# Merging the scores of two key chunks into 136 columns in a banded-attention stage

## The chip, the cores and the metric

The kernel runs on one core of a Trainium2 chip. Five engines work side by side, each in the order in which its instructions were written: TensorE (PE in the profile, its weight loads PEld), VectorE (DVE), ScalarE (ACT), GpSimd (POOL) and SyncE (SP, which issues transfers). The metric is the device time of one execution in microseconds. Three runs of the kernel before gave 881.18, 882.76 and 883.11 us; the median is 882.76.

## The reference

```python
scores = scale * np.matmul(q, k.transpose(0, 1, 3, 2))     # 2 x 8 heads, 768 x 768, head size 64
is_sink = pos[None, :] < 4
rel = pos[:, None] - pos[None, :]
keep = is_sink | ((rel >= 0) & (rel < 128))
a = softmax(np.where(keep, scores, -1e9))
attn = np.matmul(a, v)
x = attn.transpose(0, 2, 1, 3).reshape(1536, 512)
x = sum_e p[:, e] * (relu(x @ w1[e]) @ w2[e])              # 4 experts
out = gate * (relu(x @ w1b[top]) @ w2b[top])               # 8 experts, the best one for each token
```

A query sees the 128 keys up to its own and the first 4 keys. For a tile of 128 queries these lie in two chunks of 128 keys: its own chunk (key column no greater than the query's row) and the one before it (key column greater than the row).

## The kernel before

The attention stage (`narrow_path`) works on 8 pairs of heads, g = 0 to 7, and in each on 6 query tiles, i = 0 to 5, and two heads, `par` = 0 and 1. For each (g, i, par) TensorE computes the scores of 264 key columns into a PSUM bank (`scores`, line 370: the chunk before, the tile's own chunk and 8 sink columns). VectorE adds a mask and takes the row's minimum of the negated scores (`mask_max`, line 383), ScalarE takes the exponential and its sum (`exp`, line 389), VectorE makes the reciprocal (lines 402, 403), and GpSimd scales the row (`norm`, line 408; for the last pair VectorE too).

The probabilities are then transposed by TensorE, by key chunk c: `pt_pe` transposes what tile c has in its own chunk (line 415) and what tile c+1 has in that chunk (line 417), for both heads, four blocks of 128x128 for c = 0 to 4 and two for c = 5. ScalarE or VectorE copies them out of PSUM (`pt_ev`, line 420, tile `ptx`, four buffers), and `av` (line 454) multiplies them with the values. The sink columns go another way (`sink_cp`, `sink_pe`, `sink_ev`, `av_sink`). `x_hi` and `x_lo` (lines 469, 473) write the result for the experts. The transposed queries and keys of the next pair (lines 324 to 347) and a few casts of expert weights (lines 678, 682, on GpSimd) are worked in between.

What stands in which order on the engines is set by the class `Order`: every step has a rank (`RANK`, tuned numbers), a cost in microseconds per engine that may run it, and steps that it waits for; a list planner takes them one by one and writes them out. PSUM has two buffers for scores and two for transposed blocks. After the last pair TensorE goes on at once with the experts, whose order the planner does not set.

Of the kernel before, what the change touches and what calls it, by code (L numbers as in the profile page):

```python
# [19 lines left out]
P = 128  # L20
# [16 lines left out]
VAR = [0, 1, 2, 3, 2, 3]  # L37
SPLIT3 = ((0, 0), (0, 1), (1, 0))
RANK = dict(
    sc=-1.86, mask=-1.68, exp=2.32, recip=1.03, norm=5.82, scp=-0.61, spe=2.96, sev=1.51, pt=2.75, ev=6.07, av=6.4, avs=4.76, xhi=11.43,  # L40
    xlo=1.57, qpe=-6.05, qhi=-8.82, qlo=-11.56, kpe=-4.73, khi=-2.69, klo=1.91, qld=-11.4, kld=-11.4, vld=-7.72, vsl=-4, wld=0, Lpt=5.73, Lsc=-2.22,
    Lav=8.22, Lexp=-2.63, Lnorm=3.72, Lkpe=-4.67, Lavs=11.14, Lrecip=2.17, Lxlo=5.65, Lkhi=-5.14, Lxhi=9.92, Lev=6.37, Lscp=-0.42,
    Lsev=1.82,
)
SLACK = dict(PE=0.02, ACT=0.17, DVE=0.06, POOL=0, SP=0)
GROUP = ((0, 1), (1, 2), (2, 3), (3, 4), (4, 5), (5, 6))
# [160 lines left out]
class Attention:  # L207


    def __init__(s, tc, st, c0, ps, q, k, v, n_sink, window, x, ident):  # L210
# [3 lines left out]
        nc = s.nc  # L214
        c1 = st.enter_context(tc.tile_pool(name="a1", bufs=1))
# [8 lines left out]
        V, A, G = nc.vector, nc.scalar, nc.gpsimd  # L224
# [15 lines left out]
        e = c1.tile([1, 1], F32, name="warm")  # L240
# [10 lines left out]
        s.masks = c1.tile([P, 4, W], F32, name="masks")  # L251
# [5 lines left out]
        G.memset(s.masks[:, 1, 2 * P :], -1.0e30)  # L257
        s.q_pe(0, s.pp[:, 0], 0)
        s.busy(s.xo[1], 6)
        s.k_pe(0, s.xo[0], 0)  # L260
# [25 lines left out]
    def make_masks(s, pool):  # L286

        V, A, masks = s.nc.vector, s.nc.scalar, s.masks
        win = pool.tile([P, 2 * P], F32, name="win")
        snk = pool.tile([P, P], F32, name="snk")  # L290
        V.tensor_scalar(win, s.rel, s.wf, -1.0e30, ALU.is_ge, ALU.mult)
        V.tensor_scalar(snk, s.key, s.nsf, -1.0e30, ALU.is_ge, ALU.mult)
        V.tensor_tensor(masks[:, 0, :P], win[:, P:], snk, ALU.max)
        V.tensor_tensor(masks[:, 1, :P], win[:, :P], snk, ALU.max)
        A.copy(masks[:, 1, P : 2 * P], win[:, P:])
        A.copy(masks[:, 2, : 2 * P], win)
        A.copy(masks[:, 2, 2 * P :], snk[:, :NS])
        A.copy(masks[:, 3, :P], win[:, :P])
        A.copy(masks[:, 3, P : P + NS], snk[:, :NS])
        A.copy(masks[:, 3, P + NS :], win[:, P:])  # L300

    def load(s, g, n, z=slice(0, 6)):
        b, h0 = divmod(g * 2, H)
# [44 lines left out]

    def narrow_path(s, ctx, late, parts):

        tc, nc, ident = s.tc, s.nc, s.ident
        c1 = ctx.enter_context(tc.tile_pool(name="b1", bufs=1))
        vsr, pp, vt = s.vsr, s.pp, s.vt
        NP = NPAIR
        masks, sk = s.masks, s.sk
        skT = [c1.tile([P, P], F32, name=f"skT{n}") for n in range(2)]
        V, A, G = nc.vector, nc.scalar, nc.gpsimd
# [6 lines left out]
        def scores(g, i, par):  # L364
            t = pr[g]
            qs, kk = s.qs[g % 2], s.kk[g % 2].rearrange("p s a c -> p s (a c)")
            z = slice(par * HD, (par + 1) * HD)
            sc = ps1.tile([P, 512], F32, tag="sc", name="sc")
            for n, (x, y) in enumerate(SPLIT3):
                nc.tensor.matmul(  # L370
                    sc[:, :W], qs[z, x, i * P : (i + 1) * P], kk[z, y, START[i] : START[i] + W], start=(n == 0), stop=(n == 2)
                )
            t["sc", par] = sc

        def mask_max(g, i, par):
            t = pr[g]
            if i == 0 and par == 0:
                t["P"] = hp_.tile([P, 2, 6, W], F32, tag="P", name="P")
                t["nm"] = sm.tile([P, 2, 6], F32, tag="nm", name="nm")
                t["su"] = sm.tile([P, 2, 6], F32, tag="su", name="su")  # L380
            m = sm.tile([P, W], F32, tag="m", name="m")
            t["m", par, i] = m
            V.tensor_tensor_reduce(  # L383
                m, t["sc", par][:, :W], masks[:, VAR[i]], -1.0, 3.0e38, ALU.add, ALU.min, t["nm"][:, par, i : i + 1]
            )

        def exp(g, i, par):
            t = pr[g]
            A.activation(  # L389
                t["P"][:, par, i],  # L390
                t["m", par, i],
                AF.Exp,
                scale=-1.0,
                bias=t["nm"][:, par, i : i + 1],
                accum_out=t["su"][:, par, i : i + 1],
            )
# [7 lines left out]

        def norm(g, a, b, par, eng):
            t = pr[g]
            y = t["P"][:, par, a:b]
            eng.tensor_tensor(y, y, t["r", a][:, par].unsqueeze(2).to_broadcast([P, b - a, W]), ALU.mult)  # L408
# [12 lines left out]

        def pt_ev(g, c, eng):
            n = 2 * P if c < 5 else P
            px = sm.tile([P, 2, 2 * P], F32, tag="ptx", name="ptx")
            pr[g]["ptx", c] = px
            copy(eng, px[:, :, :n], pr[g]["pt", c][:, :, :n])

        def sink_cp(g):
            z, o = (slice(2, 5, 2), 256), (slice(3, 6, 2), 128)
            for i, n in (z, o):  # L430
                d = sk[g % 2][:, i.start - 2 : i.stop - 2 : 2, : 2 * NS].rearrange("p i (h n) -> p h i n", h=2)
                G.tensor_copy(d, pr[g]["P"][:, :, i, n : n + NS])
# [56 lines left out]
        for g in range(NP):  # L489
# [41 lines left out]
            add("scp", g, 0, 0, dict(POOL=0.46), lambda e, g=g: sink_cp(g), sum((normed[i] for i in range(2, 6)), [("spe", g - 2, 0, 0)]))  # L531
            add("spe", g, 0, 0, dict(PE=0.107), lambda e, g=g: sink_pe(g), [("scp", g, 0, 0)], ("pt", 2, [("sev", g, 0, 0)]))
            add("sev", g, 0, 0, dict(ACT=0.16, DVE=0.20), lambda e, g=g: sink_ev(g, E[e]), [("spe", g, 0, 0), *all_("avs", g - 2, range(2, 6))])
            for c in range(6):
                k = (g, c, 0)
                old = normed[c] + (normed[c + 1] if c < 5 else [])
                add("pt", *k, dict(PE=0.43 if c < 5 else 0.215), lambda e, g=g, c=c: pt_pe(g, c), old, ("pt", 2, [("ev", *k)]))
                cost = dict(ACT=0.48, DVE=0.60) if c < 5 else dict(ACT=0.26, DVE=0.33)
                add("ev", *k, cost, lambda e, g=g, c=c: pt_ev(g, c, E[e]), [("pt", *k)], ("ptx", 4, [("av", *k)]))
# [1005 lines left out]
```

## Time and profile before

| | us |
|---|---|
| median of three runs | 882.76 |
| the profiled execution | 883.79 |
| its span, first to last instruction | 882.0 |
| PE busy in the span | 865.5 (98%) |
| DVE, ACT, POOL busy | 403.2, 312.8, 136.0 |
| first scores of pair 0 | 9.5 |
| first matmul of the experts | 123.0 |

Times in a row of the profile count from the first instruction. A busy PE is not PE at its peak: ends of matmuls are modelled, and overlapping ones count as busy throughout. So in the attention stage TensorE is read from the distance between the starts of its instructions and from the weight loads (PEld).

### The profile page before, as it was taken

The page shows a single profiled execution, that of the slowest core. Times are in us where ns is not written, and L with a number is a line of the kernel's source. Part 1 is how long each engine was busy: PE and PEld are TensorE (multiplying, and loading weights), DVE is VectorE, ACT ScalarE, POOL GpSimd, SP SyncE. Part 2 cuts the span into 40 slices and gives each one's busy share as a digit, 9 for nine tenths or more (in the row PEclk, how much of TensorE's full clock was granted, in tenths as well). Part 3 has the DMA queues.
Part 4 walks back from the last instruction along what each step waited for, and adds up shares of the span by engine and source line. Part 5 has one row for each costly group of instructions (what it writes and reads, how often), then busy time and mean ns, then how long its engine had stood idle before and what let it go on. Part 6 is the DMA issues. An engine that isn't in the chain of part 4 may idle for free. (4 is left out here: it accounts for less than half of the span.)

```text
span 882.0 us, 11784 instructions
## 1 busy us (share of the span) xinstructions
PE 865.5 (98%) x4266; PEld 678.6 (77%) x4266; DVE 403.2 (46%) x1025; ACT 312.8 (35%) x683; POOL 136.0 (15%) x248
## 2 busy tenths in 40 slices
PE   8999999999999999999999999999999999999997
PEld 6676677878888888888888888888887677777875
DVE  5787754121234121234121234868556766826511
ACT  5887852010303010303020213121234667837522
POOL 4576510010000000000000000012131412211111
PEclk8999999999999999999999999999999999999999
DMA  7557110030033000022000020200324786946200
GB/s 137 113 136 157 37 56 2 1 121 1 0 96 94 1 1 1 1 95 72 25 1 0 1 72 25 107 13 36 132 81 137 220 296 194 331 147 194 97 34 23
DMA packets 84399, 72.45 MB, mean 82 GB/s; under 512 B 43860, under 2 KB 68436, under 8 KB 84328
## 3 DMA queue, kind: packets, MB, share of 16 engines
q1 hardware_dynamic: 81448, 65.25, 25.1%
q0 software_dynamic: 2880, 6.30, 2.1%
q8 instruction: 39, 0.64, 0.3%
q14 instruction: 32, 0.26, 0.1%
HBM read 67.58 MB, written 7.09 MB: 85 GB/s over the span
## 5 line engine op out<-in xcount | busy, mean ns | idle before, releaser
L1080 PE MATMUL po<-wA,h 128*128 128x512 f32 x1152 | 273.4, 396 | 0.0
L998 PE MATMUL ph<-x,wA 128*128 128x512 f32 x1152 | 273.0, 397 | 0.3 <-PEq L1465 0.3
L998 PEld LDWEIGHTS ph<-x,wA 128*128 128x128 f32 x1152 | 216.5, 188 | 53.0 <-issue 0.7
L1080 PEld LDWEIGHTS po<-wA,h 128*128 128x128 f32 x1152 | 215.1, 188 | 51.7
L1003 ACT ACTIVATE h<-ph 128x512 fp32r<-128x512 f32 x96 | 57.4, 598 | 388.0 <-PE ph L998 384.4
L1004 DVE SCALAR_TENSOR_TENSOR h<-ph,h 128x512 fp32r<-128x512 f32 x96 | 66.4, 692 | 174.6 <-ACT h L1003 174.6
L682 DVE TENSOR_TENSOR wA<-raw,wA 128x512 fp32r<-128x512 f32 x122 | 78.7, 685 | 2.8 <-ACT wA L676 1.8
L1090 DVE SCALAR_TENSOR_TENSOR acc<-po,pr,acc 128x512 f32<-128x512 f32 x36 | 27.0, 749 | 110.0 <-PE po L1080 110.0
L60 POOL TENSOR_TENSOR gn<-gn,rss 128x4 f32<-128x4 f32 x9 | 1.8, 199 | 444.0 <-DVE gn L58 443.6
L676 ACT CAST wA<-raw 128x512 fp32r<-128x512 f32 x124 | 70.0, 618 | 0.4 <-ACTq L1344 0.4
L408 POOL TENSOR_TENSOR P<-P,r 128x264 f32<-128x264 f32 (+1 forms) x87 | 54.2, 647 | 43.0 <-DVE r L403 22.1
L1217 PE MATMUL po<-wA,ht 128*128 128x512 f32 x216 | 56.5, 402 | 0.0
L1211 DVE TENSOR_TENSOR ht<-hT,ht 128x512 fp32r<-128x512 f32 x30 | 20.7, 691 | 73.7 <-ACT ht L1210 73.7
L389 ACT ACTIVATE P<-m,nm 128x264 f32<-128x264 f32 x96 | 49.0, 513 | 8.2 <-DVE nm L383 7.5
L1217 PEld LDWEIGHTS po<-wA,ht 128*128 128x128 f32 x216 | 39.0, 188 | 7.9
L383 DVE CUSTOM_DVE_ANT_0 m<-sc,masks 128x264 f32<-128x264 f32 x96 | 38.5, 429 | 13.3 <-PE sc L370 11.7
L1194 PE MATMUL ph<-wA,xt 128*128 128x512 f32 x168 | 42.3, 400 | 1.2 <-ACTq L1344 0.8
L682 DVE TENSOR_TENSOR wB<-raw,wB 128x512 fp32r<-128x512 f32 x64 | 40.2, 683 | 3.5 <-ACT wB L676 3.5
L771 DVE CUSTOM_DVE_ANT_0 rj<-acc,raw 128x512 f32<-128x512 f32 x64 | 40.1, 687 | 0.2
L370 PE MATMUL sc<-kk,qs 64*128 64x264 f32 x288 | 37.7, 324 | 1.1 <-DVE nm L383 1.0
L1217 PE MATMUL po<-wB,ht 128*128 128x512 f32 x144 | 38.5, 405 | 0.0
L1194 PEld LDWEIGHTS ph<-wA,xt 128*128 128x128 f32 x168 | 30.8, 188 | 9.2 <-ACTq L1344 1.6
(219 smaller groups left out, 781.0 us busy)
## 6 DMA issues: line engine op xcount, KB each, us to landing
raw<-in_moe_w_dram SPq DMA_DIRECT2D x96, 512.0 KB
vt<-in_v_dram SPq DMA_DIRECT2D x16, 192.0 KB
xs<-acc SPq DMA_DIRECT2D x12, 256.0 KB
qr<-in_q_dram SPq DMA_DIRECT2D x14, 192.0 KB
kr<-in_k_dram SPq DMA_DIRECT2D x14, 192.0 KB
raw<-en SPq DMA_DIRECT2D x4, 512.0 KB
vsr<-in_v_dram SPq DMA_DIRECT2D x64, 2.0 KB
qr<-in_q_dram SPq DMA_DIRECT2D x4, 96.0 KB
```

The lines of the kernel that those rows point to most:

```text
L383: V.tensor_tensor_reduce(m, t["sc", par][:, :W], masks[:, VAR[i]], -1.0, 3.0e38, ALU.add, ALU.min, t["nm"][:, par, i : i + 1])
L389: A.activation(t["P"][:, par, i], t["m", par, i], AF.Exp, scale=-1.0, bias=t["nm"][:, par, i : i + 1], accum_out=t["su"][:, par, i : i + 1],)
L408: eng.tensor_tensor(y, y, t["r", a][:, par].unsqueeze(2).to_broadcast([P, b - a, W]), ALU.mult)
L676: eng.copy(dst()[:, 0], r)
L682: eng.tensor_tensor(d[:, 1], r, d[:, 0], ALU.subtract)
L771: s.nc.vector.tensor_tensor_reduce(j, s.acc[:, tt], s.eb[e], 1.0, 0.0, ALU.mult, ALU.add, s.dl[:, tt, e : e + 1])
L998: s.nc.tensor.matmul(ph, s.wA.w1(a, k, f * P)[:, :P], s.x[:, b, k, tb * TB : (tb + 1) * TB], start=(n == 0), stop=(n == 11))
L1003: s.nc.scalar.activation(t[:, 0], ph, AF.Relu)
L1004: s.nc.vector.scalar_tensor_tensor(t[:, 1], ph, 0.0, t[:, 0], ALU.max, ALU.subtract)
L1080: nc.tensor.matmul(po, hs[f][:, a, t * P : (t + 1) * P], wA.w2(b, f), start=(n == 0), stop=(n == 23))
L1194: nc.tensor.matmul(ph[b], x[:, a, kk], w.w1(c, kk, b * 512), start=(kk == 0 and n == 0), stop=(kk == 3 and n == 2),)
L1217: nc.tensor.matmul(s.po[0], ht[b][:, a, c * P : (c + 1) * P], w.w2(d, f), start=(f == 0 and n == 0), stop=(f == 7 and n == 2),)
```

## The change

From the third query tile on (i > 1), the two chunks are put together before the mask. Of the own and the previous chunk's columns, exactly one of each column pair is within the window, so `copy_predicated` writes the scores of one chunk over those of the other in PSUM, where a constant triangle (`pred`) says so; mask, exponential and scaling then work on 136 columns (128 and 8 sinks) and not on 264. The transposition has two blocks for a chunk and not four (chunk 0 keeps four), and the copy out of PSUM is half as wide. Behind it GpSimd parts the block into two triangles with `affine_select`: the lower one is written into the `ptx` of the chunk before (`sel` 0), the upper one stays in place (`sel` 1). `av` is the same as before and now waits for these. The matmuls of the scores keep their 264 columns. The planner gets new costs for mask, exp, ev and sel; ranks of the other steps stay, and chunks from 1 on have `pt`, `ev` and `sel` ranked one place earlier.

```diff
+        G.tensor_scalar(s.pred[0], s.rel[:, P:], 1.0e30, None, ALU.is_ge)
+        G.tensor_scalar(s.pred[1], s.rel[:, P:], 1.0e30, None, ALU.is_lt)
...
-        A.copy(masks[:, 2, : 2 * P], win)
-        A.copy(masks[:, 2, 2 * P :], snk[:, :NS])
-        A.copy(masks[:, 3, :P], win[:, :P])
...
+        V.tensor_tensor(masks[:, 2, :P], win[:, :P], win[:, P:], ALU.max)
+        A.copy(masks[:, 2, P:MW], snk[:, :NS])
...
+            if i > 1:
+                o, z = (P, 0) if CUR[i] == P else (0, CUR[i])
+                V.copy_predicated(sc[:, o : o + P], s.pred[0 if o else 1], sc[:, z : z + P])
             V.tensor_tensor_reduce(
-                m, t["sc", par][:, :W], masks[:, VAR[i]], -1.0, 3.0e38, ALU.add, ALU.min, t["nm"][:, par, i : i + 1]
+                m, sc[:, o : o + w], masks[:, min(i, 2), :w], -1.0, 3.0e38, ALU.add, ALU.min, t["nm"][:, par, i : i + 1]
             )
...
-                nc.tensor.transpose(pt[:, par, :P], t["P"][:, par, c, CUR[c] : CUR[c] + P], ident)
-                if c < 5:
-                    nc.tensor.transpose(pt[:, par, P:], t["P"][:, par, c + 1, 0:P], ident)
+                o = P if c == 1 else 0
+                nc.tensor.transpose(pt[:, par, :P], t["P"][:, par, c, o : o + P], ident)
+                if c == 0:
+                    nc.tensor.transpose(pt[:, par, P:], t["P"][:, par, 1, 0:P], ident)
...
+        def select(g, i, part):
+            t = pr[g]
+            y = t["ptx", i][:, :, :P]
+            if part:
+                G.affine_select(out=y, in_=y, pattern=[[0, 2], [1, P]], compare_op=ALU.is_ge, fill=0.0, base=0, channel_multiplier=-1)
+            else:
+                G.affine_select(
+                    out=t["ptx", i - 1][:, :, P:], in_=y, pattern=[[0, 2], [-1, P]], compare_op=ALU.is_ge, fill=0.0, base=-1, channel_multiplier=1
+                )
...
-                    add("mask", *k, dict(DVE=0.355), ...
+                    add("mask", *k, dict(DVE=0.46 if i > 1 else 0.355), ...
-                    add("exp", *k, dict(ACT=0.50), ...
+                    add("exp", *k, dict(ACT=0.37 if i > 1 else 0.50), ...
+                    add("sel", g, c, 0, dict(POOL=0.39), ..., [("ev", *k), ("ev", g, c - 1, 0)], None, sh)
+                    add("sel", g, c, 1, dict(POOL=0.39), ..., [("sel", *k)], None, sh)
+                old += ([("sel", g, c, 1)] if c > 1 else []) + ([("sel", g, c + 1, 0)] if 0 < c < 5 else [])
```

On DVE, in pair 1, tile 2, both heads (`sc` scores, `m` masked, `nm` the row's minimum, `r` the reciprocal; an ISA row is the masking instruction, and one with `nm` alone reads its accumulator), before:

```order
L383 ISA m_501,nm_453<-sc_488,masks_165 128x264
L383 ISA nm_453 128x1
L383 ISA m_507,nm_453<-sc_497,masks_165 128x264
L383 ISA nm_453 128x1
L402 TENSOR_SCALAR r_513<-su_454 128x2
L403 RECIPROCAL r_513<-r_513 128x2
```

and now, with the semaphores that a row waits for:

```order
L389 COPY_PREDICATED sc_502<-pred0_166,sc_502 128x128 [waits PE_49]
L390 ISA m_519,nm_470<-sc_502,masks_165 128x136 [waits DVE_49]
L390 ISA nm_470 128x1
L389 COPY_PREDICATED sc_511<-pred0_166,sc_511 128x128 [waits PE_49]
L390 ISA m_525,nm_470<-sc_511,masks_165 128x136 [waits DVE_49]
L390 ISA nm_470 128x1
L409 TENSOR_SCALAR r_537<-su_471 128x2 [waits Activation_49]
```

A predicated copy stands ahead of each masking instruction, which waits for VectorE's own semaphore.

On PE, in pair 1 (`pt` transposed blocks, `ptx` their copies; `xo0` takes the output), before:

```order
L370 MATMUL sc_488<-kk1_100,qs1_98 128x264 x3
L370 MATMUL sc_497<-kk1_100,qs1_98 128x264 x3
L454 MATMUL xo0_105<-ptx_418,vt0_94 64x256 x2
L370 MATMUL sc_516<-kk1_100,qs1_98 128x264 x3
L370 MATMUL sc_521<-kk1_100,qs1_98 128x264 x3
L415 MATMUL pt_529<-ident_63,P_302 128x128
L417 MATMUL pt_529<-ident_63,P_302 128x128
L415 MATMUL pt_529<-ident_63,P_302 128x128
L417 MATMUL pt_529<-ident_63,P_302 128x128
L454 MATMUL xo0_105<-ptx_442,vt0_94 64x256 x2
```

and now:

```order
L372 MATMUL sc_502<-kk1_100,qs1_98 128x264 x3
L372 MATMUL sc_511<-kk1_100,qs1_98 128x264 x3
L471 MATMUL xo0_105<-ptx_420,vt0_94 64x256 x2
L423 MATMUL pt_529<-ident_63,P_302 128x128 x2
L372 MATMUL sc_533<-kk1_100,qs1_98 128x264 x3
L372 MATMUL sc_543<-kk1_100,qs1_98 128x264 x3
L454 MATMUL pts_551<-ident_63,sk0_163 128x128
L471 MATMUL xo0_105<-ptx_434,vt0_94 64x256 x2
```

Two transpositions stand where there were four; the first products of pair 0 still follow the scores of pair 1, tile 2.

On POOL, in pair 4 (`wA`, `raw` expert weights), before:

```order
L408 TENSOR_TENSOR P_1103<-P_1103,r_1323 128x264 x2
L682 TENSOR_TENSOR wA0_79<-raw1_72,wA0_79 128x2x256
L432 COPY sk0_163<-P_1103 128x2x2x8 x2
L408 TENSOR_TENSOR P_1353<-P_1353,r_1418 128x264 x2
L408 TENSOR_TENSOR P_1353<-P_1353,r_1466 128x264 x2
```

and now, at the cast of pair 3 that stands like it:

```order
L415 TENSOR_TENSOR P_926<-P_926,r_1165 128x136 [waits DVE_49]
L415 TENSOR_TENSOR P_926<-P_926,r_1165 128x136
L705 TENSOR_TENSOR wA0_79<-raw0_71,wA0_79 128x2x256
L449 COPY sk1_164<-P_926 128x2x4x8 [waits Pool_49]
L443 AFFINE_SELECT ptx_1162<-ptx_1208 128x2x128 [waits Activation_49]
L443 AFFINE_SELECT ptx_1208<-ptx_1234 128x2x128 [waits Activation_49]
L441 AFFINE_SELECT ptx_1208<-ptx_1208 128x2x128 [waits Pool_49]
L441 AFFINE_SELECT ptx_1234<-ptx_1234 128x2x128 [waits PE_49,Pool_49]
```

The selects stand in GpSimd's one queue, here behind an expert cast. From the last pair's `x_lo` on, every engine has the same order in both kernels.

## Rows read from the trace of the kernel before

**Rows 1.** Busy time by stretch: length, then busy us of each engine (instructions), clock, DMA.

```profile
8.00:123.00 115.00, 112.86 (x882) 78.51 (x880) 87.07 (x343) 87.96 (x266) 65.68 (x120) 0.97 0.52 110
26.00:110.00 84.00, 84.00 (x676) 58.09 (x674) 65.83 (x265) 67.48 (x203) 53.92 (x97) 1.00 0.51 112
```

**Rows 2.** Timeline at the stage's end: start us, duration us, engine, line, instruction.

```profile
122.57 0.71 PE L445 MATMUL prep<-skT,vsr 128*128 128x128 f32 x4
123.03 5.17 PE L998 MATMUL ph<-x,wA 128*128 128x512 f32 x21
```

**Rows 3.** Waits in 8:123: who waited for whom, us, times, longest.

```profile
DVE m L383 <- PE sc L370: 11.7, 21, 1.4
ACT P L389 <- DVE nm L383: 7.5, 18, 0.9
ACT ptx L420 <- PE pt L417: 6.8, 14, 1.2
POOL w L82 <- DVE fi L272: 5.3, 1, 5.3
```

**Rows 4.** Groups by line and shape, 0:122: count, busy us, mean ns, idle before.

```profile
L389 ACT ACTIVATE P<-m,nm 128x264 f32<-128x264 f32 x96 | 49.0, 513 | 8.2 <-DVE nm L383 7.5 <-POOL P L408 0.2
...
L420 ACT COPY ptx<-pt 128x512 f32<-128x512 f32 x27 | 15.7, 586 | 7.1 <-PE pt L417 6.8
...
L420 DVE COPY ptx<-pt 128x512 f32<-128x512 f32 x13 | 8.9, 683 | 3.7 <-PE pt L417 3.7
...
L420 DVE COPY ptx<-pt 128x256 f32<-128x256 f32 x6 | 2.5, 420 | 2.9 <-PE pt L415 2.9
...
L420 ACT COPY skT<-pts 128x128 f32<-128x128 f32 x7 | 1.8, 261 | 2.3 <-PE pts L437 2.3
...
L420 ACT COPY ptx<-pt 128x256 f32<-128x256 f32 x2 | 0.7, 370 | 0.0
...
L420 DVE COPY skT<-pts 128x128 f32<-128x128 f32 x1 | 0.3, 292 | 0.3 <-PE pts L437 0.3
```

**Rows 5.** The same view, the scalings, a select and the casts on POOL.

```profile
L408 POOL TENSOR_TENSOR P<-P,r 128x264 f32<-128x264 f32 x84 | 50.5, 627 | 37.6 <-DVE r L403 16.7 <-ACT P L389 8.8 <-DVE r L402 7.6
...
L682 POOL TENSOR_TENSOR wA<-raw,wA 128x512 fp32r<-128x512 f32 x4 | 5.1, 1278 | 0.0
...
L408 POOL TENSOR_TENSOR P<-P,r 128x528 f32<-128x528 f32 x3 | 3.7, 1218 | 5.4 <-DVE r L403 5.4
...
L247 POOL TENSOR_SCALAR_AFFINE_SELECT rel<-rel 128x256 f32<-128x256 f32 x1 | 0.4, 388 | 0.0
```

**Rows 6.** The same view, the transpositions of probabilities on PE.

```profile
L415 PE MATMUL pt<-ident,P 128*128 128x128 f32 x96 | 25.7, 304 | 0.0
L417 PE MATMUL pt<-ident,P 128*128 128x128 f32 x80 | 20.6, 283 | 0.0
```

**Rows 7.** Timeline of DVE, mask constants, 9.2 to 9.9.

```profile
9.24 0.30 DVE L292 TENSOR_SCALAR snk<-key,i64t 128x128 f32<-128x128 f32 x1
9.57 0.29 DVE L293 TENSOR_TENSOR masks<-win,snk 128x128 f32<-128x128 f32 x1
9.78 0.28 DVE L294 TENSOR_TENSOR masks<-win,snk 128x128 f32<-128x128 f32 x1
```

**Rows 8.** Timeline of PE, transpositions of one chunk.

```profile
51.29 0.27 PE L417 MATMUL pt<-ident,P 128*128 128x128 f32 x1
...
51.40 0.27 PE L415 MATMUL pt<-ident,P 128*128 128x128 f32 x1
...
51.51 0.27 PE L417 MATMUL pt<-ident,P 128*128 128x128 f32 x1
```

**Rows 9.** Busy time by stretch as rows 1, ahead of and within the half clock.

```profile
14.00:16.00 2.00, 1.25 (x12) 0.83 (x8) 1.79 (x7) 2.00 (x7) 2.00 (x4) 1.00 0.02 3
...
18.00:20.00 2.00, 2.00 (x9) 1.43 (x10) 1.27 (x3) 0.81 (x2) 1.47 (x3) 0.50 1.03 232
```

**Rows 10.** Tile `ptx`, window 0:40: count, min/median/max ns, first and last start.

```profile
L454 PE MATMUL xo<-ptx,vt x28: 272/379/430, 25.8 to 37.3; 128*64 128x256 f32 x16, 128*64 128x128 f32 x12
L420 ACT COPY ptx<-pt x7: 586/587/589, 19.8 to 36.5; 128x512 f32<-128x512 f32 x7
```

More of the change, by code (lines that the diff above doesn't have):

```diff
@@ L36 @@
 START = [0, 0, 128, 256, OFF[3], OFF[4]]
-VAR = [0, 1, 2, 3, 2, 3]
+MW = P + NS
+WT = [2 * P, 2 * P] + [MW] * 4
 SPLIT3 = ((0, 0), (0, 1), (1, 0))
@@ L42 @@
     Lav=8.22, Lexp=-2.63, Lnorm=3.72, Lkpe=-4.67, Lavs=11.14, Lrecip=2.17, Lxlo=5.65, Lkhi=-5.14, Lxhi=9.92, Lev=6.37, Lscp=-0.42,
-    Lsev=1.82,
+    Lsev=1.82, sel=6.2, Lsel=6.3,
 )
@@ L250, in __init__ @@
         s.sk = [c1.tile([P, 4, 32], F32, name=f"sk{n}") for n in range(2)]
-        s.masks = c1.tile([P, 4, W], F32, name="masks")
+        s.masks = c1.tile([P, 3, 2 * P], F32, name="masks")
+        s.pred = [c1.tile([P, P], I32, name=f"pred{i}") for i in range(2)]
         for t in s.sk:
@@ L256, in __init__ @@
         G.memset(s.masks[:, 0, P:], -1.0e30)
-        G.memset(s.masks[:, 1, 2 * P :], -1.0e30)
+        G.tensor_scalar(s.pred[0], s.rel[:, P:], 1.0e30, None, ALU.is_ge)
+        G.tensor_scalar(s.pred[1], s.rel[:, P:], 1.0e30, None, ALU.is_lt)
         s.q_pe(0, s.pp[:, 0], 0)
@@ L294, in make_masks @@
         V.tensor_tensor(masks[:, 1, :P], win[:, :P], snk, ALU.max)
-        A.copy(masks[:, 1, P : 2 * P], win[:, P:])
-        A.copy(masks[:, 2, : 2 * P], win)
-        A.copy(masks[:, 2, 2 * P :], snk[:, :NS])
-        A.copy(masks[:, 3, :P], win[:, :P])
-        A.copy(masks[:, 3, P : P + NS], snk[:, :NS])
-        A.copy(masks[:, 3, P + NS :], win[:, P:])
+        A.copy(masks[:, 1, P:], win[:, P:])
+        V.tensor_tensor(masks[:, 2, :P], win[:, :P], win[:, P:], ALU.max)
+        A.copy(masks[:, 2, P:MW], snk[:, :NS])
     def load(s, g, n, z=slice(0, 6)):
@@ L368, in scores @@
             sc = ps1.tile([P, 512], F32, tag="sc", name="sc")
+            w = W if i > 1 else 2 * P
             for n, (x, y) in enumerate(SPLIT3):
                 nc.tensor.matmul(
-                    sc[:, :W], qs[z, x, i * P : (i + 1) * P], kk[z, y, START[i] : START[i] + W], start=(n == 0), stop=(n == 2)
+                    sc[:, :w], qs[z, x, i * P : (i + 1) * P], kk[z, y, START[i] : START[i] + w], start=(n == 0), stop=(n == 2)
                 )
@@ L389, in exp @@
             A.activation(
-                t["P"][:, par, i],
+                t["P"][:, par, i, : WT[i]],
                 t["m", par, i],
@@ L406, in norm @@
             t = pr[g]
-            y = t["P"][:, par, a:b]
-            eng.tensor_tensor(y, y, t["r", a][:, par].unsqueeze(2).to_broadcast([P, b - a, W]), ALU.mult)
+            y = t["P"][:, par, a:b, : WT[a]]
+            eng.tensor_tensor(y, y, t["r", a][:, par].unsqueeze(2).to_broadcast([P, b - a, WT[a]]), ALU.mult)
         def pt_pe(g, c):
@@ L422, in pt_ev @@
         def pt_ev(g, c, eng):
-            n = 2 * P if c < 5 else P
+            n = P if c else 2 * P
             px = sm.tile([P, 2, 2 * P], F32, tag="ptx", name="ptx")
@@ L426, in pt_ev @@
             copy(eng, px[:, :, :n], pr[g]["pt", c][:, :, :n])
+        def select(g, i, part):
[7 more added lines that the diff above has]
+                )
         def sink_cp(g):
[L429 to L432, printed above, removed]
+            d = sk[g % 2][:, :, : 2 * NS].rearrange("p i (h n) -> p h i n", h=2)
+            G.tensor_copy(d, pr[g]["P"][:, :, 2:, P:MW])
         def sink_pe(g):
@@ L477, in narrow_path, with add @@
         R = RANK
-        def add(name, g, i, par, cost, fn, after=(), buf=None):
+        def add(name, g, i, par, cost, fn, after=(), buf=None, shift=0):
             r = R.get("L" + name, R[name]) if g == NP - 1 else R[name]
-            order.add((name, g, i, par), 6 * g + i + r + 0.1 * par, cost, fn, after, buf)
+            order.add((name, g, i, par), 6 * g + i - shift + r + 0.1 * par, cost, fn, after, buf)
         def all_(name, g, i=range(6), par=(0,)):
@@ L517, in narrow_path @@
                     add("sc", *k, dict(PE=0.335), lambda e, k=k: [scores(*k), k == NOTED and s.note()], split, ("sc", 2, [("mask", *k)]))
-                    add("mask", *k, dict(DVE=0.355), lambda e, k=k: mask_max(*k), [("sc", *k)], ("m", 4, [("exp", *k)]))
+                    add("mask", *k, dict(DVE=0.46 if i > 1 else 0.355), lambda e, k=k: mask_max(*k), [("sc", *k)], ("m", 4, [("exp", *k)]))
                     old = [*all_("pt", g - 2), ("scp", g - 2, 0, 0)] if i == 0 else []
-                    add("exp", *k, dict(ACT=0.50), lambda e, k=k: exp(*k), [("mask", *k), *old])
+                    add("exp", *k, dict(ACT=0.37 if i > 1 else 0.50), lambda e, k=k: exp(*k), [("mask", *k), *old])
             normed = {}
@@ L524, in narrow_path @@
                 for par in AB:
-                    cost = dict(POOL=0.12 + 0.46 * (b - a))
+                    n = (b - a) * WT[a] / W
+                    cost = dict(POOL=0.12 + 0.46 * n)
                     if g == NP - 1:
-                        cost["DVE"] = 0.06 + 0.28 * (b - a)
+                        cost["DVE"] = 0.06 + 0.28 * n
                     add("norm", g, b - 1, par, cost, lambda e, k=(g, a, b, par): norm(*k, E[e]), [("recip", g, b - 1, 0)])
@@ L530, in narrow_path @@
                     normed[i] = all_("norm", g, [b - 1], AB)
-            add("scp", g, 0, 0, dict(POOL=0.46), lambda e, g=g: sink_cp(g), sum((normed[i] for i in range(2, 6)), [("spe", g - 2, 0, 0)]))
+            add("scp", g, 0, 0, dict(POOL=0.25), lambda e, g=g: sink_cp(g), sum((normed[i] for i in range(2, 6)), [("spe", g - 2, 0, 0)]))
             add("spe", g, 0, 0, dict(PE=0.107), lambda e, g=g: sink_pe(g), [("scp", g, 0, 0)], ("pt", 2, [("sev", g, 0, 0)]))
@@ L535, in narrow_path @@
                 k = (g, c, 0)
[L536 to L539, printed above, removed]
+                old = normed[c] + ([] if c else normed[1])
+                sh = 1 if c else 0
+                add("pt", *k, dict(PE=0.215 if c else 0.43), lambda e, g=g, c=c: pt_pe(g, c), old, ("pt", 2, [("ev", *k)]), sh)
+                cost = dict(ACT=0.26, DVE=0.36) if c else dict(ACT=0.48, DVE=0.60)
+                add("ev", *k, cost, lambda e, g=g, c=c: pt_ev(g, c, E[e]), [("pt", *k)], ("ptx", 4, [("av", *k)]), sh)
+                if c > 1:
+                    add("sel", g, c, 0, dict(POOL=0.39), lambda e, g=g, c=c: select(g, c, 0), [("ev", *k), ("ev", g, c - 1, 0)], None, sh)
+                    add("sel", g, c, 1, dict(POOL=0.39), lambda e, g=g, c=c: select(g, c, 1), [("sel", *k)], None, sh)
                 old = [("ev", *k), ("vld", g, 0, 0)] + ([("av", g, c - 1, 0)] if c else [])
+                old += ([("sel", g, c, 1)] if c > 1 else []) + ([("sel", g, c + 1, 0)] if 0 < c < 5 else [])
                 if c in (0, 2):
```

6 lines of the change are left out of this document (4 added, 2 removed).

## The prediction

> **What bounds the kernel now.** I read the table of busy time by stretch first, then the end of the stage in the timeline, then the waits, then the groups by line. Only the attention stage is touched. It lasts from about 8 to 123 us, 115 us, and the rest has the same order on every engine. At its end the last matmul of attention starts at 122.57 and the experts' first at 123.03, and TensorE goes on with them at once [rows 2]; so what the stage gains or loses is gained or lost by the kernel, microsecond for microsecond.
>
> In the stage no engine is full. VectorE is busy for 87.07 and ScalarE for 87.96 of the 115 us, 76% each; GpSimd for 65.68, and TensorE's weight loads, which I read in place of its modelled matmuls, for 78.51, 68% [rows 1]. The waits say how the rest comes about: VectorE waits 11.7 us for scores, ScalarE 7.5 us for masked rows and 6.8 us for transposed blocks [rows 3]. It is a chain through four engines in fixed order, with VectorE and ScalarE the fullest; neither is full enough that its work alone sets the time.
>
> **The change, part by part.** It touches tiles 2 to 5 of 8 pairs and two heads, 64 units of 96, and 40 copies out of PSUM.
>
> ScalarE, exponentials. One of 264 columns takes 513 ns. The copies of 512 and 256 columns take 586 and 370 ns, 0.844 ns a column [rows 4], so 128 columns fewer save 108 ns, and 64 of them 6.9 us.
>
> Copies out of PSUM. Before, ScalarE has 27 of 512 columns and 2 of 256 (27 x 0.586 + 2 x 0.370 = 16.6 us), VectorE 13 and 6 (13 x 0.683 + 6 x 0.420 = 11.4 us) [rows 4]. In the new order ScalarE has 7 and 31 (15.6), VectorE 1 and 9 (4.5): ScalarE saves 1.0, VectorE 6.9. Four of the copies of sink columns go from ScalarE to VectorE: 4 x 261 ns less on the one, 4 x 292 ns more on the other, 1.0 and 1.2 us [rows 4].
>
> VectorE, masks. The masking instruction loses 128 columns; by its copies (683 less 420 ns over 256 columns, 1.03 ns a column [rows 4]) that is 132 ns. The predicated copy of 128 columns that comes before it is not in this trace. Low end: two instructions of 128 columns with no wait between them start 0.21 us apart, lines 293 and 294. High end with a wait: where the second waits for the first on the same engine, lines 292 and 293, it is 0.33 us [rows 7]. Net 0.08 or 0.20 us for a unit, 5.1 or 12.8 us in all. Farther up: if the copy, which also has its destination as an operand, made a second pass over its 128 columns, 0.13 us more, 21 us in all. Below nothing it can't be, since a whole instruction is added for half of one. In the new order the masking row waits for VectorE's own semaphore each time, so the pair of lines 292 and 293 is nearest: I take 12.8.
>
> In these two rows 0.13 of the 0.21 or 0.33 us goes to the columns, and 0.08 or 0.20 is fixed, paid by each instruction anew [rows 7]. [...]
>
> Sum of the two: ScalarE -6.9 - 1.0 - 1.0 = -8.9; VectorE +12.8 - 6.9 + 1.2 = +7.1; together -1.8 of 175.0 us. (Three scalings of the last pair on VectorE become narrower too, well under a microsecond, not counted.)
>
> TensorE. Of 176 transpositions of probabilities [rows 6] 112 are left: with 264 columns, 8 pairs x 22, now 8 x 14. Within a chunk they start 0.11 us apart [rows 8], so 64 fewer save 7.0 us. The scores' matmuls are not narrower.
>
> GpSimd. A scaling of 264 columns takes 627 ns, of 528 columns 1218, 2.24 ns a column [rows 5]; 128 fewer save 287 ns, 64 x 0.287 = 18.4 us. 64 selects of 256 elements come in; the one select of that size takes 388 ns [rows 5], 24.8 us. Net +6.4 us on 65.7. What hides it: GpSimd is idle for over 49 of the stage's 115 us [rows 1]. What hides the selects' latency: in pair 0 the first copy of a transposed block starts at 19.8 and the first product with it at 25.8 [rows 10], 6 us against two selects of 0.39. If that cover is gone, a select and what stands ahead of it in GpSimd's queue is on the path (third rival).
>
> At nothing: the predicates on GpSimd at the start, two small instructions, lie in its 5.3 us of waiting for `fi` [rows 3]; the narrower sink copies lie in GpSimd's idle time. What is late next: after ScalarE's relief, VectorE's masks are what ScalarE waits for.
>
> **The sum.** The stage's length follows the work of the engines on its chain, at the idle share that it has now. By VectorE and ScalarE alone: 115 x 1.8 / 175.0 = 1.2 us less. With TensorE's loads as the third: 115 x (1.8 + 7.0) / (175.0 + 78.5) = 4.0 us less. The chain goes through all three, but TensorE is the least full, so I take the middle, 2.6 us. The profiled execution took 883.79 us (its span is 882.0, and 1.8 lies around it): 883.8 - 2.6 = 881.2. It was 1.03 us over the median of the runs, 882.76, so the runs should give 880.1.
>
> **Rivals.**
>
> VectorE becomes the bound (slower). It is to carry 94.2 us where it carried 87.1. If its idle 27.9 us [rows 1] stay, since the static order still makes it wait for scores, blocks and `x`, the stage grows by the whole 7.1: 889.9. It decides where less than 7.1 us of that idle time go. For it: the predicated copy stands in the loop of two score buffers, and the next scores can't start until it and the mask are through; the ranks of the other steps are as they were for other costs. Against it: 11.7 us of the idle time are waits for scores [rows 3], which a longer mask of the other buffer partly covers, and VectorE loses the copies out of PSUM, which wait too. At the far end of the copy's cost (21 us) it would carry 15 us more.
>
> TensorE is what the chain really turns on (faster). Then the stage loses its 7.0 us of transpositions: 875.8. For it: VectorE's longest wait is for PE's scores, ScalarE's copies wait 6.8 us for PE [rows 3]. Against it: the loads are busy for only 68%.
>
> GpSimd comes onto the path (slower). The casts of expert weights, 1278 ns each, four of them [rows 5], stand in the same queue; three of the four have selects close behind them in the new order. If products wait for those, 3 x 1.28 = 3.8 us come in against the 1.2 that VectorE and ScalarE save: 885.4. Against it: the 6 us of cover.
>
> A second stretch at half clock (no change). [...] One more such stretch of some 7 us costs at most half its length, 3.4: 883.5. [...] Against it: from 26 to 110 us the clock stays at 1.00 [rows 1] with loads at 69%.
>
> **How the numbers follow.** Chances: the forecast 0.40 (its own range, 1.2 to 4.0 us less, 881.5 to 878.7), VectorE as the bound 0.28, TensorE 0.14, GpSimd 0.08, the clock 0.07, and 0.03 for effects that cancel. About 0.2%, 1.8 us, is what a measurement of this kernel can tell from no change. Of the forecast's 0.40, 0.09 lies within that. Faster: 0.31 + 0.14 = 0.45; same: 0.09 + 0.07 + 0.03 = 0.19; slower: 0.28 + 0.08 = 0.36. Cases of both signs hold most of it, so the range goes from a little past the TensorE case, 874.5, to VectorE's at its price, 889.5.
>
> **What would show it.** In the new profile: predicated copy and mask start 0.33 us apart, so that a unit has 0.20 us more on VectorE than before; an exponential of 136 columns 405 ns; a select 388 ns; VectorE busy for about 94 us of the stage and ScalarE for 79; the experts' first matmul at 120 to 121 us. It is wrong if a unit gains under 0.1 us (then more is gained) or over 0.3, if VectorE's idle time in the stage stays near 28 us, if products wait for selects for more than 2 us in total, or if the clock row shows half clock after 26 us.

## The result: 0.9% slower

| | us |
|---|---|
| before, median of 20 runs | 884.62 (880.68 to 887.62) |
| after, median of 20 runs | 894.45 (884.83 to 902.20) |
| ratio | 1.009, 95% interval 1.0068 to 1.0112 |
| after, the profiled execution, its span | 895.07, 893.4 |

The forecast was 880.1, in 874.5 to 889.5. The ratio is of the means and leaves out three slow runs of after (898.13, 902.01, 902.20). Four runs of after stand apart, at 884.83 to 885.05 and a mean granted clock of 0.996 to 0.998. The other 16 took 891.65 or more, 15 of them at 0.969 to 0.988; one took 897.75 at 0.999, so the clock does not account for every long run, and no trace of that one is kept. The profiled run was at 0.979. The same program once more (experiment a_again) took 885.20 at 0.996. So the loss has two parts, and these two traces of one program part them.

The stage's end, answering to [rows 2], in the timeline of after:

```profile
136.83 0.71 PE L462 MATMUL prep<-skT,vsr 128*128 128x128 f32 x4
137.30 0.48 PE L1021 MATMUL ph<-x,wA 128*128 128x512 f32 x1
```

and of the same program once more:

```profile
127.09 0.71 PE L462 MATMUL prep<-skT,vsr 128*128 128x128 f32 x4
127.56 0.48 PE L1021 MATMUL ph<-x,wA 128*128 128x512 f32 x1
```

The experts begin at 137.30 and 127.56, before at 123.03 [rows 2]; what follows takes 756 us in both, and 759 in before's trace, which has one more stretch of half clock there (3.4 us at 689 us). So both parts lie in the attention stage.

**Part one, the clock.** Busy time by stretch (length, then PE, PEld, DVE, ACT, POOL, granted clock), after:

```profile
5.00:8.60 3.60, 1.60 (x21) 1.34 (x20) 1.56 (x9) 0.88 (x2) 0.00 (x0) 1.00 0.76 142
9.00:12.00 3.00, 3.00 (x18) 2.09 (x16) 2.20 (x10) 0.91 (x3) 2.10 (x9) 0.50 1.38 220
12.00:18.00 6.00, 5.13 (x23) 3.99 (x23) 3.68 (x19) 4.15 (x14) 2.21 (x4) 0.50 0.52 64
18.00:22.00 4.00, 4.00 (x19) 2.82 (x20) 1.94 (x10) 1.79 (x7) 0.90 (x3) 0.50 1.16 236
22.00:43.00 21.00, 20.83 (x91) 14.28 (x90) 13.30 (x63) 11.26 (x41) 9.41 (x23) 0.50 0.38 70
```

and the same program once more:

```profile
5.00:8.60 3.60, 1.54 (x21) 1.28 (x20) 1.55 (x9) 0.89 (x2) 0.00 (x0) 1.00 0.77 141
9.00:12.00 3.00, 3.00 (x18) 2.11 (x16) 2.09 (x9) 0.91 (x3) 2.11 (x9) 0.50 1.38 222
12.00:18.00 6.00, 5.16 (x33) 3.82 (x33) 5.40 (x27) 4.66 (x16) 2.33 (x4) 1.00 0.54 67
18.00:22.00 4.00, 4.00 (x23) 2.98 (x23) 3.22 (x15) 3.14 (x11) 1.57 (x4) 0.61 1.16 235
22.00:43.00 21.00, 20.65 (x147) 14.07 (x146) 16.06 (x72) 15.45 (x53) 14.17 (x35) 0.99 0.57 122
```

Read the clock, third from the right. Both fall to half (0.50) at 8.6 to 8.7 after the same thin stretch (PE busy 1.6 of 3.6 us). One recovers within 3.4 us, and falls once more for 3.4; the other stays down for 34.1 us without a break. From pair 2's first scores on they agree again: 90.3 us (47.0 to 137.3) and 90.4 (37.2 to 127.6). So 27.3 us more at half clock cost 9.7. The experts of after begin 14.3 us later than before's: 9.7 by the clock, 3.9 from pair 2 on at full clock, and 0.7 ahead of pair 2.

**Part two, at like clock.** a_again's 885.2 at 0.996 stands against 880.12 to 882.37 of before's runs at 0.995 and 0.996, and from pair 2's first scores to the experts, at full clock, the change takes 90.4 us where before took 86.5 (36.5 to 123.03). Most of what was forecast of the engines came about; after, groups by line (count, busy, mean ns, idle before them), answering to [rows 4 to 6]:

```profile
L396 ACT ACTIVATE P<-m,nm 128x136 f32<-128x136 f32 x64 | 26.1, 409 | 11.8 <-DVE nm L390 11.2
L423 PE MATMUL pt<-ident,P 128*128 128x128 f32 x96 | 22.4, 316 | 0.6 <-ACT ptx L428 0.6
L415 POOL TENSOR_TENSOR P<-P,r 128x136 f32<-128x136 f32 x56 | 22.0, 413 | 21.7 <-DVE r L410 16.8 <-ACT ptx L428 4.6 <-ACT P L396 0.4
L390 DVE CUSTOM_DVE_ANT_0 m<-sc,masks 128x136 f32<-128x136 f32 x64 | 19.1, 299 | 2.8
L389 DVE COPY_PREDICATED sc<-pred,sc 128x128 f32<-128x128 int32 x64 | 18.6, 291 | 17.2 <-PE sc L372 16.4 <-issue 0.4
L441 POOL TENSOR_SCALAR_AFFINE_SELECT ptx<-ptx 128x256 f32<-128x256 f32 x32 | 13.1, 419 | 0.4
```

The exponential takes 409 ns (forecast 405), a select 419 (388), a scaling 413 (627 less 287, so 340), and the row of the predicated copy ends in its wait, 16.4 us for TensorE's scores. The waits, answering to [rows 3], say the same of a_again:

```profile
DVE sc L389 <- PE sc L372: 8.6, 13, 1.8
ACT x L486 <- PE xo L462: 6.3, 9, 1.7
DVE m L390 <- PE sc L372: 5.1, 8, 1.6
```

VectorE waits for scores for 13.7 us, before for 11.7 [rows 3], so it is TensorE that is late. One reason shows in its timeline, here of a_again (start, duration, instruction; x6 are both heads' scores of a tile, x3 one head's):

```profile
68.80 0.63 PE L372 MATMUL sc<-kk,qs 64*128 64x264 f32 x6
69.36 0.44 PE L423 MATMUL pt<-ident,P 128*128 128x128 f32 x2
...
72.92 0.64 PE L372 MATMUL sc<-kk,qs 64*128 64x264 f32 x3
73.48 0.71 PE L462 MATMUL xo<-skT,vsr 128*128 128x128 f32 x4
74.12 0.64 PE L372 MATMUL sc<-kk,qs 64*128 64x264 f32 x3
74.69 0.65 PE L471 MATMUL xo<-ptx,vt 128*64 128x256 f32 x4
```

Six matmuls of two heads hold TensorE for 0.56 us, and so do three of one head. By these lines a score has 64*128 of the array where a transposition has 128*128, so a head uses 64 of its rows. Scores of two heads that stand next to each other can start in pairs: in after's trace six matmuls start at 68.518 and 68.528, 68.744 and 68.754, 68.865 and 68.875, and three of one head alone at 65.250, 65.477 and 65.594. So two heads side by side run together, and a head that stands alone costs as much as both. By the starts of the matmuls from pair 2's first scores on, at full clock, in before and in after alike, matmuls of one array shape follow each other after 0.109 us, and where the shape changes after 0.205 (medians): a change costs 0.10 us more. In the order of before 13 heads stand alone, in the change 25.

To see what this is worth I summed the distances of TensorE's starts from pair 2's first scores to the experts. A run of matmuls of one kind and number needs what the shortest of such runs take over nine traces (the lowest twentieth); I call this work and what is beyond it waiting. Where the runs are grouped in another way, the differences between two kernels move by up to 2 us from work to waiting; the sums stay.

| us | work | waiting | sum |
|---|---|---|---|
| before | 74.1 | 12.4 | 86.5 |
| the change (a_again) | 71.3 | 19.1 | 90.4 |

In the work, transpositions are down from 17.5 to 11.0 and scores up from 22.7 to 26.7; the waiting grows by 6.7. Whom it is for is shown in part: in this stretch the waits that the profile lists for the weight loads come to 23.7 us, before to 18.7. What ends with GpSimd is up from 0.8 to 3.5 us, mostly its selects; for 12.1 (before 11.6) the profile names nobody.

### The profile page after: what moved, and what is told of

Read it like the earlier page. It is cut to its first block, busy times and chain, and to the rows that moved or that the text cites. A ratio compares the mean times of both kernels' runs of the same rounds, so it can differ in the third digit from the quotient of the medians.

```text
span 893.4 us, 11840 instructions
## 1 busy us (share of the span) xinstructions
PE 874.3 (98%) x4202; PEld 682.2 (76%) x4202; DVE 407.3 (46%) x1085; ACT 303.6 (34%) x684; POOL 146.5 (16%) x305
## 5 line engine op out<-in xcount | busy, mean ns | idle before, releaser
L372 PE MATMUL sc<-kk,qs 64*128 64x264 f32 (+1 forms) x288 | 47.7, 352 | 2.1 <-DVE nm L390 2.0
L396 ACT ACTIVATE P<-m,nm 128x136 f32<-128x136 f32 (+1 forms) x96 | 42.2, 441 | 13.6 <-DVE nm L390 13.0
L415 POOL TENSOR_TENSOR P<-P,r 128x136 f32<-128x136 f32 (+3 forms) x87 | 41.1, 495 | 29.7 <-DVE r L410 20.2
L372 PEld LDWEIGHTS sc<-kk,qs 64*128 64x128 f32 x288 | 33.4, 217 | 15.9 <-issue 5.6
```

The source lines that it names most:

```text
L372: nc.tensor.matmul(sc[:, :w], qs[z, x, i * P : (i + 1) * P], kk[z, y, START[i] : START[i] + w], start=(n == 0), stop=(n == 2))
L396: A.activation(t["P"][:, par, i, : WT[i]], t["m", par, i], AF.Exp, scale=-1.0, bias=t["nm"][:, par, i : i + 1], accum_out=t["su"][:, par, ...
```

## The experiments

Times are medians; each ratio is to before, measured beside it on the same chip (medians 884.81, 884.87 and 884.89 us). Where the experts begin in the traces of four of them:

```profile
136.45 0.77 PE L1021 MATMUL ph<-x,wA 128*128 128x512 f32 x1
130.11 0.48 PE L1020 MATMUL ph<-x,wA 128*128 128x512 f32 x1
118.09 0.48 PE L998 MATMUL ph<-x,wA 128*128 128x512 f32 x1
139.59 0.48 PE L998 MATMUL ph<-x,wA 128*128 128x512 f32 x1
```

These are a_tr4, a_tr4_nocp, b_sc2 and b_split, in this order.

**a_again**: the change, unedited.

> The changed kernel once more, for a second profile. Theory C (TensorE's clock): the long stretch at half clock at the start of the attention stage (8.7 to 42.9 us in the first profile) is what makes most of the loss, so executions without it take about 885 us (granted clock 0.996 or more) and those with it 892 to 902; a second profile with another length of half clock has its first matmul of the experts earlier or later by about 0.3 to 0.4 us for each microsecond of half clock. Theory V (VectorE's masks or the planner's order): the stage has the same length, about 129 us, whatever the clock row says.

885.20 us, told above: one program, two clocks, and 0.36 us for each microsecond of half clock, as theory C had it.

**a_tr4**: the change with 64 transpositions that nothing uses, in the places that before has them.

```diff
-                if c == 0:
-                    nc.tensor.transpose(pt[:, par, P:], t["P"][:, par, 1, 0:P], ident)
+                if c < 5:
+                    nc.tensor.transpose(pt[:, par, P:], t["P"][:, par, 1 if c == 0 else c, 0:P], ident)
```

> The changed kernel with 64 transpositions more, unused: for chunks 1 to 4 TensorE again makes four blocks into the half of the PSUM tile that nothing reads. Order and all else are as in the change. Theory C: TensorE is as active as before the change, the half clock at the start ends about where it did before (7 us long, and not 34), and the time falls from 894 to 884 to 887, although TensorE has 7 us more to do. Theory V: nothing gets faster; 894 or, with 7 us of transpositions partly on the path, up to 899.

894.61 us, 1.012 (1.0091 to 1.0149). From pair 2 to the experts 95.7 us (40.8 to 136.45) against 90.4, with 2.2 us of half clock in it, which costs at most 1.1. So 4.2 to 5.3 us come out at the end, of the 5.3 that 48 transpositions add there at 0.11 each: TensorE has next to no slack. Theory C held for the clock (10.2 us of half clock at the start and not 34.1; no run under 0.984) and failed for the time. The median is that of after by coincidence: less half clock, more transpositions. Theory V's number came out, but VectorE is not the reason, as the next run shows.

**a_tr4_nocp**: a_tr4 without the predicated copy; the mask works on one chunk's scores, so the other chunk is left out of the softmax.

```diff
-                V.copy_predicated(sc[:, o : o + P], s.pred[0 if o else 1], sc[:, z : z + P])
```

> As a_tr4, and the predicated copy is left out (the mask then works on one chunk's scores alone): 64 instructions of 0.325 us fewer on VectorE, 20.8 us. Theory V: VectorE's masks are the price, so the stage loses most of these, 10 us or more against a_tr4. Theory C: at the same clock VectorE, which is busy for 72% of the stage, is not what it turns on; 2 to 6 us less than a_tr4.

889.11 us, 1.0064 (1.004 to 1.0087), 5.5 less than a_tr4. From pair 2 to the experts it is 2.5 less (93.2 us from 36.9 on, against 95.7), of which the clock in a_tr4 may be 1.1; most of the rest lies ahead of pair 2, where it has 3.4 us of half clock and a_tr4 10.2. The 48 copies left out from pair 2 on, 0.325 us of VectorE's queue each, are 15.6 us, so at most a sixth of VectorE's work counts. It is not the bound here. In the change itself, with fewer transpositions on TensorE, this was not tried.

**b_sc2**: before with two of three products of each score (the low part of the queries is left out).

```diff
-            for n, (x, y) in enumerate(SPLIT3):
+            for n, (x, y) in enumerate(SPLIT3[:2]):
```

> The kernel before with two of the three products of each score (the product of the queries' low part with the keys' high part is left out): 96 matmuls of 264 columns fewer, about 5 us less for TensorE, and nothing else changed. Theory C: the start of the stage is now thin for TensorE as in the change, the half clock lasts tens of microseconds there in most executions, and the kernel gets slower, 888 to 896. Theory V: VectorE and the order are as before, so 882 to 885, or a few us faster where scores are waited for.

879.47 us, 0.9936 (0.9912 to 0.996); 81.9 us from pair 2 to the experts, 4.6 less than before: the 5 us less that were expected of TensorE's work come out at the end in before too. Theory C failed: with less work the half clock at the start lasted 10.2 us (before 6.8), not tens of microseconds.

**b_split**: before with the second head's scores ranked later, so that 53 heads stand alone, not 13.

```diff
-            order.add((name, g, i, par), 6 * g + i + r + 0.1 * par, cost, fn, after, buf)
+            order.add((name, g, i, par), 6 * g + i + r + (0.6 if name == "sc" else 0.1) * par, cost, fn, after, buf)
```

> The kernel before, and in the planner the second head's scores rank 0.6 of a tile later and not 0.1: its order then has 53 heads alone and 18 tiles side by side (13 and 38 before). No work is added on any engine. Theory S: 40 heads alone more at 0.56 us and 20 tiles side by side fewer at 0.58 are about 10 us more for TensorE, so 892 to 897. Theory V: VectorE and ScalarE have the same work, so 884 to 888.

899.50 us in four runs, 1.0168 (1.012 to 1.0216), 14.6 slower, with the same work in another order. From pair 2 to the experts, at full clock, it takes 98.5 us (41.1 to 139.59) against 86.5; of the 12.0, the distances after scores' matmuls carry 9.5 (33.1 against 23.6). The rest lies at the start, where its trace has 17.1 us of half clock and before's 6.8. Theory S holds in its mechanism; its 892 to 897 left out the clock.

**a_pair**, **b_pair**: the change, and before, with both heads' scores as one step.

```diff
+                    if par == 0:
+                        add("sc", *k, dict(PE=0.57), lambda e, k=k: [scores(*k), scores(k[0], k[1], 1), ...], split, ("sc", 1, [("mask", g, i, 0), ("mask", g, i, 1)]))
```

> The change, with the scores of both heads of a tile as one step of the planner (so that TensorE always gets them one behind the other; cost 0.57 for the two). In the traces so far, six matmuls of two heads next to each other hold TensorE for 0.58 us in the kernel before, and three of one head alone for 0.56; the change has 25 heads alone where the kernel before had 13. Theory S (TensorE is full from its first scores on, and the change lost the side-by-side scores of two heads): with all 48 tiles side by side the experts start 7 to 10 us earlier than in the changed kernel at like clock, at 117 to 121 us instead of 127.6, and the kernel takes 874 to 879 without a long half clock. Theory V (VectorE's longer masks): VectorE's work is the same, so no more than 2 us are gained, 883 or more.

> The kernel before with the scores of both heads as one step in the same way. Theory S: it had 13 heads alone and two longer runs, so 2 to 4 us are gained, 880 to 882 beside 884.8. Theory V: nothing to gain, 884 to 886; a new order may cost a few us more.

**a_pair_cal**: a_pair with the measured costs in the planner (`mask` 0.55, `exp` 0.405).

> As a_pair, and the planner's costs are those that the traces show: 0.55 for predicated copy and mask together (0.46 in the change) and 0.405 for the shorter exponential (0.37). Theory S: TensorE's order has the same 48 tiles side by side, so about the time of a_pair, 2 us up or down. Theory P (the planner's wrong cost of the masks makes engines wait for each other): 3 us or more less than a_pair.

890.60 us (1.0081, 1.0055 to 1.0108), 887.54 (1.0044, 1.0017 to 1.0071) and 891.27 (1.008, 1.0055 to 1.0105). Pairing alone did not pay, and theory S was wrong on a_pair by 11 us or more: TensorE's work fell (a_pair_cal 62.9 us, b_pair 70.2), and its waiting rose (29.4, of which at most 1.7 is a stretch of half clock, and 19.3). The measured costs changed little, so theory P failed too. The ranks were tuned for other steps. Hence the last four, in which the ranks and slacks were sought anew for four kernels in one way: a model of the engines' queues, fitted to six of these traces, ranked the candidate orders.

**a_rank**, **b_rank**: the change and before, with new `RANK` and `SLACK` alone.

> The change with other ranks and slacks, and nothing else; in this order both heads' scores of a tile stand side by side for all 48 tiles (before: 13 heads stand alone, in the change 25), and TensorE changes its array shape 183 times (before 180, the change 195). Theory A: what the change lost at full clock lies in the order, in which ranks tuned for other costs parted the heads and made TensorE wait; the idea itself takes 64 transpositions, 5 to 7 us, off TensorE, which is nearly full. Then the experts begin at 115 to 121 us (before 123.0, the change at a short half clock 127.6), the time is 876 to 882, and the same ranks' work on the kernel before gives less: a_rank is 3 to 8 us ahead of b_rank. Theory B: the predicated copy and the selects lengthen the chain from a score to its product whatever the order. Then a_rank stays at 884 or more, and behind b_rank by 3 us or more.

> The control: the kernel before with ranks and slacks that were sought anew in the same way and with the same effort as a_rank's; one head stands alone, 176 changes of array shape (180 before). Theory A (the loss is in the order): it gains from the pairing, some 12 heads of 0.25 us, 3 us and no transpositions, so 880 to 885, 3 to 8 us behind a_rank. Theory B (the change's chain costs in any order): 880 to 885 as well, but ahead of a_rank.

**ap_rank**, **bp_rank**: the same for a_pair_cal and b_pair.

> The change with both heads' scores as one step (a_pair_cal) and ranks and slacks sought anew: all 48 tiles paired, 143 changes of array shape, the fewest of all. a_pair_cal had the least TensorE work (64.7 us between pair 2's scores and the experts, 73.2 in the change) and the most waits (27.5 us, 17.2). Theory A (the waits come from ranks that were tuned for another kernel): with new ranks at least half of the 10 us of added waits go, so 10 to 15 us less than a_pair_cal, 876 to 882, level with a_rank or ahead by up to 4. Theory B (one step that takes both score buffers makes TensorE wait for VectorE's masks in any order): 888 to 892 as a_pair_cal had, behind a_rank.

> The control to ap_rank: the kernel before with both heads' scores as one step (b_pair, 887.5) and ranks and slacks sought anew with the same effort; 162 changes of array shape. Theory A: its waits go too, but the 64 transpositions stay on TensorE: 878 to 884, 3 to 7 us behind ap_rank. Theory B: 886 to 890, since the wait for both masks is in the step and not in the ranks; level with ap_rank or ahead of it.

| | median us | ratio to before | work | waiting |
|---|---|---|---|---|
| a_rank (change) | 881.41 | 0.9963 (0.9936 to 0.9991) | 65.8 | 17.8 |
| b_rank (before) | 880.85 | 0.9947 (0.9918 to 0.9976) | 73.4 | 11.7 |
| ap_rank (change, heads as one step) | 876.96 | 0.9919 (0.989 to 0.9948) | 64.2 | 14.8 |
| bp_rank (before, heads as one step) | 882.24 | 0.9971 (0.9945 to 0.9998) | 72.9 | 11.8 |

The end of ap_rank's stage in its timeline:

```profile
118.07 0.49 PE L462 MATMUL prep<-skT,vsr 128*128 128x128 f32 x2
118.31 0.48 PE L1022 MATMUL ph<-x,wA 128*128 128x512 f32 x1
```

and pieces of it, both heads' scores 0.57 us apart from what follows, with nothing idle ahead:

```profile
60.33 0.64 PE L372 MATMUL sc<-kk,qs 64*128 64x264 f32 x6
60.90 0.66 PE L471 MATMUL xo<-ptx,vt 128*64 128x128 f32 x8
...
62.54 0.62 PE L372 MATMUL sc<-kk,qs 64*128 64x256 f32 x6
63.11 0.55 PE L338 MATMUL prep<-ident,kr 128*128 128x128 f32 x3
```

(The row with 64x256 is a score of tile 0 or 1: in the change these have 256 columns, and only those from tile 2 on keep 264.)

Theory A holds in half of it. With nothing changed but the order, the change goes from 894.45 to 881.41 and is 0.4% faster than before: its loss went with the order, and most of the clock's part with it (13.7 us of half clock in a_rank's trace, 34.1 in after's). But b_rank gains as much without the change; a_rank was to be 3 to 8 us ahead of it and is level. From pair 2 on its work is 7.6 us less and its waiting 6.1 more, so what the transpositions save is given back in waiting. That the longer way from a score to its product makes these waits, as theory B has it, is my reading and was not tried by itself; the loads' waits that end with GpSimd, 2.3 us in a_rank and none in b_rank, fit it but do not fill it. With both heads as one step the change is 5.3 us ahead of its control, as theory A had it: 8.7 less work, 3.0 more waiting. Theory B is out for the paired scores: with new ranks ap_rank's waiting is half of a_pair_cal's. ap_rank beats both kernels shown, by 0.8% and by about 2%. One search for each is thin ground for differences of a microsecond or two; that a_rank and b_rank are equal may lie in the search.

## Why the prediction was wrong

- **"In the stage no engine is full", "TensorE is the least full".** This step failed. TensorE was nearly full, and the forecast held it for the engine with most room. I read TensorE by its weight loads, 68%, and took them for its load. The matmuls' row, 84.00 busy in 84 us [rows 1], I put aside as modelled. Loads show neither the 0.56 us that one head's three matmuls hold the array for, nor a change of the array's shape: 0.205 us against 0.109. a_tr4 (4.2 to 5.3 of 5.3 us), b_sc2 (4.6 of about 5) and b_split (12.0) show TensorE's work at the end for nearly its full price. The share that I chose as the middle of the sum (115 us times saved work over three engines' work) had no ground. Put right alone, this step would have made the forecast faster. The loss came from what the sum had at nothing: TensorE's new order (parted heads and waiting, 10.7 us against 6.5 saved on transpositions; with smaller items 3.9 net from pair 2 on) and the longer half clock (9.7).
- **TensorE's term, 7.0 us for 64 transpositions:** right in size (6.5 of them from pair 2 on; a_tr4 adds them back), and it did reach the path. It was not all of TensorE's term: the parted heads add 4.0, in an order of which I had read the pairs of scores in one place and not counted them.
- **What is late next.** I named VectorE's masks. It was TensorE itself, waiting 6.7 us more in an order whose ranks had been tuned for other costs (for whom is shown only in part); that the ranks stayed as they were stood in my first rival as a remark, without a price.
- **VectorE as the bound (0.28).** The median came out 4.6 us over its 889.9, and not by its way. Its price was right: copy to mask 0.32 us, a unit 0.55 us (62.16 to 62.71 in the timeline of a_again below) against 0.36 before (50.85 to 51.21), 0.19 more and not 0.20. It carries 90.9 us, not 94.2, and its idle time of 27.9 [rows 1] did stay in a_again, at 28.6; but a_tr4_nocp took 20.8 us off VectorE for 5.5 of time, part of it the clock's, and 13.7 us of the idle time are waits for TensorE's scores.

```profile
62.16 0.29 DVE L389 COPY_PREDICATED sc<-pred,sc 128x128 f32<-128x128 int32 x1
62.48 0.30 DVE L390 CUSTOM_DVE_ANT_0 m<-sc,masks 128x136 f32<-128x136 f32 x1
62.71 0.08 DVE L390 DVE_READ_ACCUMULATOR2_ANT nm<- 128x1 f32 x1
62.71 0.29 DVE L389 COPY_PREDICATED sc<-pred,sc 128x128 f32<-128x128 int32 x1
```

and of before:

```profile
50.85 0.43 DVE L383 CUSTOM_DVE_ANT_0 m<-sc,masks 128x264 f32<-128x264 f32 x1
51.21 0.08 DVE L383 DVE_READ_ACCUMULATOR2_ANT nm<- 128x1 f32 x1
51.21 0.43 DVE L383 CUSTOM_DVE_ANT_0 m<-sc,masks 128x264 f32<-128x264 f32 x1
```

The stage of a_again as a whole, answering to [rows 1] (ScalarE's 78.63 is the 79 of the forecast):

```profile
8.00:127.56 119.56, 114.14 (x821) 77.06 (x820) 90.92 (x404) 78.63 (x267) 75.67 (x176) 0.97 0.49 106
```

- **The second stretch at half clock (0.07).** It came, and its size was off: 27.3 us more at a granted clock of 0.50, and not 7 (before's own lasted 6.8 us, a part of it in [rows 9]), for 9.7 us and not 3.4. It began at the start of the stage, which I had held to be settled by before's trace, and ran to 42.9, past the 26 us that I had named as a sign.
- **GpSimd on the path (0.08).** In small part: at the last pair's products the loads of a_again wait 2.4 us for selects, just over the 2 us that I had set, and 2.8 in all, where before they waited 1.8 for other things; 1 us is new there, and from pair 2 on 2.7 us more of the loads' waits end with GpSimd. GpSimd carries 10.0 us more (75.67 against 65.68), not 6.4: a narrower scaling saves 214 ns, not 287. The group of these loads:

```profile
L471 PEld LDWEIGHTS prep<-ptx,vt 128*64 128x64 f32 x28 | 1.5, 135 | 2.8 <-POOL ptx L441 1.4 <-POOL ptx L443 1.0
```

and before:

```profile
L454 PEld LDWEIGHTS prep<-ptx,vt 128*64 128x64 f32 x28 | 1.6, 136 | 1.8 <-DVE x L473 0.7 <-ACT ptx L420 0.5 <-issue 0.2
```

- **Smaller readings.** Of the copies out of PSUM 32 become narrower, not 40; the sum used the right counts. The base of three runs, 882.76, was 1.9 us under the median of 20.

## What to carry to other kernels

Read an in-order engine by the distance between its starts, and make sure of its slack by adding work that nothing uses; a share of busy loads is not a load (68% here, on an engine that was nearly full). A change that alters the costs under a tuned order has to be tuned again, and so has its control, before one says what the idea is worth: here the order was worth 13 us of the change, the clock's part with it, and 4 of the kernel before. A difference between two programs of this kind needs many runs, since one and the same program took 885 or 895.

## What the hardware showed that I had not expected

- The granted clock of one and the same program, after the same thin stretch, came back after 3.4 us in one execution and after 34.1 in another. 16 of 20 runs of after took 891.65 us or more; ap_rank's ten lie within 874.17 to 877.75. Less work for TensorE alone did not bring the long half clock about (b_sc2, 10.2 us), and more of it went with a shorter one (a_tr4, 10.2). What decides it was not settled.
- The granted clock is not all of the spread: of the runs of before, beside the experiments, at 0.997 to 0.999, ten took 878.77 to 880.57 us and 13 took 885.10 to 887.70, with nothing between. No trace of these is kept, and the cause is open.
- Scores of two heads run fully side by side: 0.56 us for six matmuls, 0.56 for three (a_again).
- A predicated copy of 128 columns within PSUM takes 291 ns and holds what depends on it for 0.32 us: the 0.13 us more that a second pass over its columns would have cost do not show.
